# A planned order of work with a cap on open load requests and with new costs for some steps

## The chip, the cores and the metric

The kernel runs on one core of one Trainium2 chip. A core has five engines that this text names: TensorE (PE in the profile; PEld is its weight load), VectorE (DVE), ScalarE (ACT), GpSimd (POOL) and SyncE (SP), which issues DMAs. Each engine runs its own list of instructions in order, and waits for other engines through semaphores. The metric is the time of one execution on the device in microseconds (us). Before the change the median of three runs is 549.18 us (548.54 to 549.64).

## The reference

Cosine attention over 8 batches, 12 heads, 448 tokens and a head width of 64, followed by a mixer with a low-rank step over the tokens and an MLP over 768 channels:

```
q_n = q / (norm(q) + 1e-6);  k_n = k / (norm(k) + 1e-6)
attn = softmax(q_n @ k_n.T / tau);  x = attn @ v          # per head, then heads side by side: [8, 448, 768]
u = x + (x.T @ U @ V).T                                   # U [448, 32], V [32, 448]
out = u + relu(u @ w_ch1) @ w_ch2                         # 768 -> 3072 -> 768
```

Inputs and output are float32.

## The kernel before, in words

**Attention.** The batches are done one after another, in thirds of four heads and in pairs of heads. For a third, GpSimd issues one load of q and one of k (`load_qk`, line 588) into a ring of three, later two, buffers. `squares` (line 629) squares two heads at a time, on ScalarE (line 636), VectorE (line 640) or, for one third of batch 0, GpSimd (line 638), and VectorE sums each row of 64 (line 644). ScalarE and VectorE make the inverse norms (lines 658 to 666), VectorE multiplies q and k by them (line 712), and from batch 2 on a DMA transpose issued by SyncE (line 728) turns them. TensorE makes scores in bursts of three (line 776), ScalarE takes the exponentials (line 794), TensorE multiplies with v (line 821), and VectorE divides by the row sums (lines 852 and 853). v is loaded by GpSimd into two buffers, one for the even and one for the odd batches; from batch 1 on that takes six loads of line 611 and four of line 616, queued behind the six q and k loads of the same batch. A load of v waits for the values products of the batch that used the buffer before.

**Mixer and MLP.** TensorE projects (line 936) and expands (line 989), VectorE adds (line 998), and the tiles u of 128 tokens go to device memory and come back transposed through SyncE's queue. The MLP takes the first four tiles plainly (lines 1377 and 1419) and the other 24 in pairs with a scheme of seven block products in place of eight. For the first six pairs the first layer is plain (line 1265) and the second layer has seven products (line 1294); for the last six pairs both have (lines 1158 and 1294). The sums of blocks that the scheme needs are made by VectorE: of the second weights (`minus`), of the first weights (`rows_`, lines 1117 to 1120), of u (`cols_`), of the hidden layer (`sums_of`, `last_sums`), and of the products that lie in PSUM banks (line 1312). In each pair GpSimd adds u to a copy of one product for three blocks (line 1319), after ScalarE has made the copy (line 1317), and VectorE adds banks to these.

**What sets the order.** The order of the instructions on every engine is worked out while the kernel is built, by `Plan.run`. Each step is an `Op` with an engine (or a choice such as `"ACT/DVE"`), a cost in us, steps that it depends on, buffers that it takes (`acq`) and gives back (`rel`), and a priority. TensorE and GpSimd have several streams; a stream keeps its own order, and at each moment the first stream in a fixed ranking whose next step is ready is served. GpSimd's ranking is `pool_y` (the adds of line 1319), `pool_x`, `pool_q` (all loads), `pool_s`. TensorE ranks attention above the MLP. VectorE, ScalarE and SyncE take the ready step of lowest priority number; ScalarE leaves a `fast` step with a choice alone while VectorE is free:

```
if e == "ACT" and o.fast and "/" in o.eng and free["DVE"] <= t + 1e-9:
    continue
```

A load costs 0.71 us of GpSimd and ends later: the planner has one queue for loads, adds the load's `busy` time to it, and then its `late` time (`LATE` is 6.0 us; 11.0 for q and k from batch 3 on):

```
dma[q] = max(dma[q], o.end) + work
o.end = dma[q] + fixed
```

Buffers come from a `Ring`; one is free when the step that gave it back last has ended in the plan. When the planner is done, the instructions are written out in its order. The planner's times themselves are not in the program, and the waits between engines come from the data in the tiles. In batch 0, idle time that the plan shows for TensorE is filled with products that nobody reads (line 698).

Of the kernel before, what the change touches and what calls it, by code (L numbers as in the profile page):

```python
# [126 lines left out]

class Slot:
    def __init__(self, ring, uses):
        self.ring, self.uses, self.left, self.i, self.tile, self.last = ring, uses, uses, None, None, 0.0  # L130


class Op:
# [8 lines left out]
class Plan:  # L142
# [53 lines left out]
    def run(self):  # L196
# [26 lines left out]
        while left:  # L223
# [6 lines left out]
            while progress:  # L230
                progress = False
                for e in ("PE", "ACT", "POOL", "DVE", "SP"):
# [65 lines left out]
                                s.group = s.ring.take(s.i, t)  # L298
                    for s in o.rel:
                        s.left -= 1  # L300
                        s.last = max(s.last, o.end)
                        if s.left == 0:
                            s.ring.freed[s.i] = s.last
                    for c in kids.pop(o.seq, ()):
# [13 lines left out]
def kernel(  # L318
# [12 lines left out]
    nc = tc.nc  # L331
# [193 lines left out]
    def any_t(n, fast=1, fixed=0.065):  # L525
        return {"ACT": act_t(n), "DVE": dve_t(n, fast, fixed)}

    def load(fn, busy, deps=(), acq=(), rel=(), late=2.0):
        return plan.add(Op("POOL", 0.71, fn, deps=deps, acq=acq, rel=rel,
                           lat=("in", busy, late)), pool_q)  # L530

    def fill(fn, n=256, prio=8, acq=(), deps=()):
# [52 lines left out]
    def load_qk(b, h0, h1, ld=None, lo=0, uses=None):  # L585

        ld = ld or Slot(r_ld, 4 if uses is None else uses)
        ops = [load(lambda i=i, src=src: nc.gpsimd.dma_start(  # L588
            out=ld.tile[:, i, lo:lo + h1 - h0, :],
            in_=src[b, h0:h1].rearrange("h (s c) d -> s h (c d)", c=SC)),  # L590
            (h1 - h0) * (0.31 if b else 0.35) + (FIRST.get((h0, i), 0.0) if b == 0 else 0.0), acq=[ld], late=2.5 if b == 0 else LATE if b < 3 else 11.0) for i, src in enumerate((q, k))]
        return ld, ops, lo

    def key_rows(n0, n1):
# [8 lines left out]
    def load_v(b):  # L603

        old = [last_av.get((b - 2, p)) for p in range(NPAIR)] + (v_set[b] if WIDE <= b < WIDE + 2 else [])
        src = v[b].rearrange("h (s c) d -> c s h d", c=SC)
        if b < WIDE:
            ops = [load(lambda c=c: nc.gpsimd.dma_start(out=v_t[b % 2][0:SCH, :, c, 0:D], in_=src[c]),
                        SCH * H * 0.001, deps=old, late=LATE if b else VLATE) for c in range(SC)]
        else:  # L610
            ops = [load(lambda j=j, r0=r0, c=c, s0=s0, s1=s1: nc.gpsimd.dma_start(  # L611
                out=v_t[b % 2][r0:r0 + s1 - s0, :, j, 0:D], in_=src[c, s0:s1]),
                (s1 - s0) * H * 0.001, deps=old, late=LATE) for j, r0, c, s0, s1 in key_rows(0, 384)]
            (_, _, c, s0, s1), = key_rows(384, S)
            for e, hh in ((0, 0), (0, 1), (1, 0), (1, 1)):
                ops.append(load(lambda e=e, hh=hh, c=c, s0=s0, s1=s1: nc.gpsimd.dma_start(
                    out=v_t[b % 2][64 * e:64 * e + 64, 2 * e + hh::4, SC - 1, 0:D],
                    in_=src[c, s0:s1, 2 * e + hh::4]),
                    (s1 - s0) * H * 0.00025, deps=old, late=LATE))
        for h in range(H):  # L620
            got[b, h, "v"] = ops

    def squares(b, g, ld, ops, lo, ii, ss, pr, on, hold, then):

        red = []
        for i in ii:
            for a0 in range(0, g, G // 2):
                a1 = min(g, a0 + G // 2)
                sq = Slot(r_sq, 1)
                o = Op(on, 1.02 if on == "POOL" else 0.48 if on == "ACT" else 0.44, None,  # L630
                       deps=[ops[i], *hold], acq=[sq], prio=pr + 0.2, fast=True, port=True)
# [17 lines left out]
        return red  # L649
# [108 lines left out]
    def scores(b, slots, then=()):  # L758
# [26 lines left out]
        for (p, c), sc, (attn, exps) in zip(slots, scs, into):  # L785
            _, _, (inv, a, scaled) = sets[p]
            if (b, p) in RAW_KEYS:
# [12 lines left out]
    def values(b, p, X):  # L800
# [39 lines left out]
        for hh in range(2):  # L840
# [259 lines left out]
    def seven_rows(after, free):  # L1100
# [26 lines left out]
    def up_seven(tiles, relu, tops, ready, left, made_by, qk_free, s_free, z_free):  # L1127
# [8 lines left out]
            return qk_t[:, 384 * n:384 * (n + 1)].rearrange("p (i t) -> p i t", i=3)  # L1136

        def cols_(f, deps):
            return plan.add(Op("DVE", 0.15 + 384 * 0.00053, f, deps=deps, acq=[uT.slot], prio=-0.6, port=True))
# [49 lines left out]
        for k in (1, 6, 2, 7, 5, 3, 4):  # L1189
            for g in range(len(gs)):  # L1190
# [20 lines left out]
                elif k == 3:  # L1211
                    o = product(3, g, C_, False, [x["q22"]])
                    x["q12"] = op("DVE", PS, sum_op(blocks(g, 1), wide(z12[g]), C_, True), [o, x["z12"]], [relu], [z12[g], C_])
                    x["r12"] = op("DVE", 0.28, lambda g=g: nc.vector.tensor_relu(out=blocks(g, 1)(), in_=blocks(g, 1)()),
                                  [x["q12"]], prio=-0.4)
                else:
                    o = product(4, g, B_, False, [x["z22"]])
# [12 lines left out]
    def sums_of(js, relu, ready, r11, r12, r21, r22):  # L1230
# [2 lines left out]
        x = slice(js[0], js[-1] + 1)  # L1233

        def sums(f, deps, prio=0.1):
            return plan.add(Op("DVE", 0.15 + len(js) * 128 * 0.00053, f, deps=deps, acq=[relu], prio=prio, port=True))
# [6 lines left out]
    def last_sums(ready, *done):  # L1243

        Q, (S1, S2) = relu_views()
        for j0, o in zip((0, HF // 2), done):
            x = slice(j0, j0 + 6)
            d = plan.add(Op("DVE", 0.15 + 6 * 128 * 0.00053, lambda x=x: nc.vector.tensor_sub(
                S1[:, x], Q[:, x, 2], S2[:, x]), deps=[o, *(ready[j][6] for j in range(j0, j0 + 6))], prio=-0.55, port=True))
            for j in range(j0, j0 + 6):  # L1250
                ready[j][3] = d
# [1 line left out]
    def mlp_seven(tiles, right, made_by, up=None, after=()):  # L1253
# [52 lines left out]
        u1, u2 = us  # L1306

        def dve(f, deps, acq=(), rel=()):
            return plan.add(Op("DVE", 0.5, f, deps=deps, acq=acq, rel=rel, prio=-0.7))

        def bank(out, x, mm):
            return lambda: nc.vector.tensor_add(out=out(), in0=mm.tile[:, 0:CH], in1=x())
# [343 lines left out]
```

## Time and profile before

| | us |
|---|---|
| median of the runs | 549.18 (548.54 to 549.64) |
| the profiled execution, its own time | 548.87 |
| its span, first to last instruction | 547.1 |
| busy: TensorE, VectorE, ScalarE, GpSimd | 537.1, 448.3, 286.5, 141.3 |

The granted clock of TensorE is 1.000 over the span. One line of a group of instructions names the source line, the engine, the operation, what it writes and reads, the shapes, the count, then busy time and the mean of one in ns, then the engine's idle time just before them and what ended it. A line of the timeline gives the start, the duration, the engine, the line and the operation, with the number of instructions merged into it, and in brackets the engine's idle time before and its releaser. In the part on DMA issues the last number is the median time from issue to landing. The time of an instruction includes its latency, and the next one on the same engine can start before it has ended; the busy time of TensorE is modelled. A step of the program that begins at 100 us is at 100 us from the first instruction.

### The profile page before, as it was taken

How to read it: one execution, taken by the hardware profiler on the slowest of the kernel's cores; microseconds unless marked ns; L12 is line 12 of the kernel's file. 1: busy time of each engine (PE TensorE's matmuls, PEld its weight loads, DVE VectorE, ACT ScalarE, POOL GpSimd, SP SyncE). 2: the span in 40 equal slices, each digit the busy share in tenths (PEclk: the TensorE clock that was granted, in tenths of full speed). 3: DMA queues.
4: the chain of work that ended last, by engine and by line, in shares of the span. 5: the costliest groups of instructions: out<-in, count | busy, mean ns of one | idle time of the engine just before them, and what ended most of it. 6: DMA issues, size and time to landing. Idle time of an engine off the chain costs nothing.

```text
span 547.1 us, 15168 instructions
## 1 busy us (share of the span) xinstructions
PE 537.1 (98%) x6275; PEld 389.2 (71%) x6275; DVE 448.3 (82%) x1022; ACT 286.5 (52%) x470; POOL 141.3 (26%) x180
## 2 busy tenths in 40 slices
PE   7899999999999999999999999999999999999996
PEld 6565565677858757757757757868778787878783
DVE  8979959999897779979979987778968585858583
ACT  7976746566557765765765765542323131314140
POOL 8636233104220620621531430010202021111111
PEclk9999999999999999999999999999999999999999
DMA  9999999987947995986996593132041212122201
GB/s 154 201 206 137 204 204 185 157 119 106 127 119 118 109 162 105 165 140 111 125 179 128 94 153 85 44 80 57 19 139 30 87 32 88 30 87 32 81 8 59
DMA packets 142326, 61.11 MB, mean 112 GB/s; under 512 B 101009, under 2 KB 142257, under 8 KB 142257
## 3 DMA queue, kind: packets, MB, share of 16 engines
q0 software_dynamic: 72352, 25.73, 43.5%
q1 hardware_dynamic: 69904, 34.41, 28.7%
q8 instruction: 49, 0.80, 0.6%
q14 instruction: 21, 0.16, 0.1%
HBM read 56.93 MB, written 15.93 MB: 133 GB/s over the span
## 4 chain that ended last, share of the span: by engine, by line
PE 92%; DVE 5%; ACT 1%; POOL 1%; DMA 1%; issue 0%; DVEq 0%; POOLq 0%
PE bank L1294 29%; PE bank L1265 18%; PE bank L1158 15%; PE bank L821 8%; PE bank L776 6%; PE bank L1377 6%; PE bank L1419 6%; PE bank L989 2%; DVE qk_all L712 2%; DVE ss L644 1%; PE bank L936 1%; POOL sqk L638 1%; DMA relu<-in_q_dram 1%; PE bank L566 1%; DVE X_sb L859 0%
## 5 line engine op out<-in xcount | busy, mean ns | idle before, releaser
L794 ACT ACTIVATE attn<-bank 128x896 bf16<-128x896 f32 (+1 forms) x163 | 140.3, 916 | 40.6 <-PE bank L776 39.7
L1294 PEld LDWEIGHTS <-relu 128*128 128x128 bf16 x1008 | 95.9, 98 | 68.4 <-issue 8.8
L1265 PE MATMUL bank<-uT,w_sb 128*128 128x256 bf16 x864 | 103.4, 273 | 0.0
L1294 PE MATMUL bank<-w_sb,relu 128*128 128x384 bf16 x576 | 102.9, 326 | 0.0
L1265 PEld LDWEIGHTS <-w_sb 128*128 128x128 bf16 x864 | 81.9, 98 | 18.1 <-issue 7.6
L644 DVE TENSOR_REDUCE ss<-sqk 112x8 f32<-112x512 bf16 x96 | 62.3, 674 | 1.1 <-ACT sqk L636 0.7
L712 DVE TENSOR_TENSOR qk_all<-qk_all,inv 112x512 bf16<-112x512 bf16 x93 | 62.5, 707 | 0.2
L821 PEld LDWEIGHTS <-attn 128*128 128x128 bf16 (+1 forms) x1536 | 54.1, 97 | 6.7 <-issue 3.7
L588 POOL DMA_DIRECT2D qk_all<-in_q_dram x24 | 17.5, 728 | 158.8 <-ACT attn L794 79.2
L821 PE MATMUL bank<-v_nat,attn 128*128 128x65 bf16 (+1 forms) x1536 | 57.3, 193 | 0.9 <-DVE X_sb L859 0.7
L1158 PEld LDWEIGHTS <-w_sb 128*128 128x128 bf16 x864 | 49.3, 98 | 0.8
L1275 ACT ACTIVATE relu<-bank 128x512 bf16<-128x512 f32 x46 | 27.5, 597 | 41.1 <-PE bank L1265 39.2
L776 PE MATMUL bank<-sqk 64*64 64x448 bf16 (+1 forms) x460 | 46.9, 356 | 0.9 <-ACT sqk L1441 0.5
L1195 ACT COPY attn<-bank 128x512 f32<-128x512 f32 x18 | 10.5, 585 | 71.0 <-PE bank L1158 69.9
L1158 PE MATMUL bank<-uT,w_sb 128*128 128x128 bf16 x648 | 38.1, 219 | 0.0
L1186 ACT ACTIVATE relu<-relu 128x512 bf16<-128x512 bf16 x36 | 22.7, 630 | 29.5 <-DVE relu L1180 28.6
L636 ACT ACTIVATE sqk<-qk_all 112x512 bf16<-112x512 bf16 x55 | 33.6, 631 | 7.5 <-DVE ss L644 7.4
L611 POOL DMA_DIRECT2D v_nat<-in_v_dram x42 | 31.1, 750 | 17.8 <-DMA w_sb<-in_moe_w_ch_dram 12.9
L1377 PE MATMUL bank<-uT,w_sb 128*128 128x384 bf16 (+1 forms) x288 | 35.4, 273 | 0.0
L1419 PE MATMUL bank<-w_sb,relu 128*128 128x384 bf16 x192 | 35.0, 326 | 0.0
L853 DVE TENSOR_TENSOR X_sb<-bank,rd 128x256 bf16<-128x256 f32 x72 | 30.6, 425 | 2.5
L998 DVE TENSOR_TENSOR X_sb<-bank,X_sb 128x384 bf16<-128x384 f32 (+3 forms) x57 | 29.2, 543 | 0.9 <-PE bank L989 0.5
(132 smaller groups left out, 794.6 us busy)
## 6 DMA issues: line engine op xcount, KB each, us to landing
qk_all<-in_q_dram POOLq DMA_DIRECT2D x23, 224.0 KB, 5.7
qk_all<-in_k_dram POOLq DMA_DIRECT2D x23, 224.0 KB, 6.7
u_nat<-u SPq DMA_DIRECT2D x25, 192.0 KB, 3.0
w_sb<-in_moe_w_ch_dram POOLq DMA_DIRECT2D x4, 1152.0 KB, 18.4
w_sb<-in_moe_w_ch_dram POOLq DMA_DIRECT2D x8, 576.0 KB, 15.9
u<-X_sb SPq DMA_DIRECT2D x22, 192.0 KB, 1.9
v_nat<-in_v_dram POOLq DMA_DIRECT2D x11, 168.0 KB, 8.4
out_dram<-O_sb SPq DMA_DIRECT2D x11, 168.0 KB, 2.5
```

The source lines that it names most:

```text
L611: ops = [load(lambda j=j, r0=r0, c=c, s0=s0, s1=s1: nc.gpsimd.dma_start(out=v_t[b % 2][r0:r0 + s1 - s0, :, j, 0:D], in_=src[c, s0:s1]), (s ...
L636: nc.scalar.activation(out=y, in_=x, func=AF.Square)
L644: lambda i=i, a0=a0, a1=a1, sq=sq: nc.vector.reduce_sum(ss.tile[:, i, a0:a1, :].rearrange("p h c -> p (h c)"), sq.tile[:, 0:a1 - a0, :].re ...
L712: (nc.gpsimd if pool_ else nc.vector).tensor_mul(dst, src, sc)
L776: nc.tensor.matmul(out=out, lhsT=qkT.tile.rearrange("p b s -> p (b s)")[r, n0:n0 + w], rhs=qkT.tile[r, SC:2 * SC, :].rearrange("p c s -> p ...
L794: exps.append(plan.add(Op("ACT", act_t(2 * S, 0.08), lambda sc=sc, c=c, attn=attn: nc.scalar.activation(out=attn.tile[:, :, off:off + S] i ...
L821: nc.tensor.matmul(out=av.tile[:, t, 0:D + 1], lhsT=tail.tile[:, hh, 128 * t:128 * (t + 1)] if tail and j == SC - 1 else (attn if j < SC - ...
L1158: o = plan.add(Op("PE", pe_t(128), lambda i=i, j=j, jj=jj: nc.tensor.matmul(out=mm.tile[:, 128 * jj:128 * jj + 128], lhsT=left[k](i, j), r ...
L1265: o = plan.add(Op("PE", pe_t(256), lambda j=j, e=e, cc=cc, mm=mm: nc.tensor.matmul(out=mm.tile[:, 256 * e:256 * e + 256], lhsT=w1_sb[:, cc ...
L1294: o = plan.add(Op("PE", pe_t(CH), lambda j=j: nc.tensor.matmul(out=mm.tile[:, 0:CH], lhsT=left[k](j), rhs=right[k](j), start=(first and j ...
L1377: o = plan.add(Op("PE", pe_t(n), lambda cc=cc: nc.tensor.matmul(out=mm.tile[:, m:m + n], lhsT=w1_sb[:, cc, f * 128:(f + 1) * 128], rhs=uT. ...
L1419: nc.tensor.matmul(out=mm.tile[:, 0:c1 - c0], lhsT=relu.tile[:, f, i * 128:(i + 1) * 128], rhs=w2_t[:, f, c0:c1], start=(f == 0), stop=(f ...
```

## The change

It touches the planner's inputs. From batch 3 on, each load of q, k and v also takes one of eight slots of a new ring, `r_turn`, and gives it back when it ends. The slots have no tile. For q and k loads the slot counts as given back 5.0 us (`late - LATE`) before the load's own end, through the new field `soon`; for v loads the two ends are the same. Then the costs of some steps are other numbers: a square 0.52 us on ScalarE (0.48 before) and 0.34 on VectorE (0.44); an exponential has a fixed part of 0.058 (0.08); dividing by the row sums 0.55 (0.6); and the block sums of the seven-product scheme are all shorter.

```
 class Slot:
     def __init__(self, ring, uses):
-        self.ring, self.uses, self.left, self.i, self.tile, self.last = ring, uses, uses, None, None, 0.0
+        self.ring, self.uses, self.left, self.i, self.tile, self.last, self.soon = ring, uses, uses, None, None, 0.0, 0.0
...
-                        s.last = max(s.last, o.end)
+                        s.last = max(s.last, o.end - s.soon)
...
-    def load(fn, busy, deps=(), acq=(), rel=(), late=2.0):
-        return plan.add(Op("POOL", 0.71, fn, deps=deps, acq=acq, rel=rel,
+    r_turn = Ring(8, None)
+
+    def load(fn, busy, deps=(), acq=(), rel=(), late=2.0, b=0):
+        turn = [Slot(r_turn, 1)] if b >= 3 else []
+        for s in turn:
+            s.own, s.soon = True, max(0.0, late - LATE)
+        return plan.add(Op("POOL", 0.71, fn, deps=deps, acq=[*acq, *turn], rel=[*rel, *turn],
                            lat=("in", busy, late)), pool_q)
...
-                o = Op(on, 1.02 if on == "POOL" else 0.48 if on == "ACT" else 0.44, None,
+                o = Op(on, 1.02 if on == "POOL" else {"ACT": 0.52, "DVE": 0.34} if "/" in on else 0.52 if on == "ACT" else 0.34, None,
...
-            exps.append(plan.add(Op("ACT", act_t(2 * S, 0.08), lambda sc=sc, c=c, attn=attn: nc.scalar.activation(
+            exps.append(plan.add(Op("ACT", act_t(2 * S, 0.058), lambda sc=sc, c=c, attn=attn: nc.scalar.activation(
...
-                muls.append(plan.add(Op("DVE", 0.6, scale, deps=[o], acq=[rd, X], rel=[av, rd], prio=1)))
+                muls.append(plan.add(Op("DVE", 0.55, scale, deps=[o], acq=[rd, X], rel=[av, rd], prio=1)))
...
-            return plan.add(Op(eng, N * 0.00203 if eng == "POOL" else 0.15 + N * 0.00053, lambda: f(e), deps=deps, prio=prio,
+            return plan.add(Op(eng, N * 0.00203 if eng == "POOL" else 0.055 + N * 0.00053, lambda: f(e), deps=deps, prio=prio,
```

The three calls in `load_qk` and `load_v` (batches from 1 on) pass `b=b`. The remaining edits are of the kind of the last two: the fixed part of `cols_` 0.15 to 0.07, of `sums_of` 0.15 to 0.09, of `last_sums` 0.15 to 0.07, a relu on VectorE 0.28 to 0.21, and the additions of banks (`dve`) 0.5 to 0.48.

More of the change, by code (lines that the diff above doesn't have):

```diff
@@ L590, in load_qk @@
             in_=src[b, h0:h1].rearrange("h (s c) d -> s h (c d)", c=SC)),
-            (h1 - h0) * (0.31 if b else 0.35) + (FIRST.get((h0, i), 0.0) if b == 0 else 0.0), acq=[ld], late=2.5 if b == 0 else LATE if b < 3 else 11.0) for i, src in enumerate((q, k))]
+            (h1 - h0) * (0.31 if b else 0.35) + (FIRST.get((h0, i), 0.0) if b == 0 else 0.0), acq=[ld], late=2.5 if b == 0 else LATE if b < 3 else 11.0, b=b) for i, src in enumerate((q, k))]
         return ld, ops, lo
@@ L612, in load_v @@
                 out=v_t[b % 2][r0:r0 + s1 - s0, :, j, 0:D], in_=src[c, s0:s1]),
-                (s1 - s0) * H * 0.001, deps=old, late=LATE) for j, r0, c, s0, s1 in key_rows(0, 384)]
+                (s1 - s0) * H * 0.001, deps=old, late=LATE, b=b) for j, r0, c, s0, s1 in key_rows(0, 384)]
             (_, _, c, s0, s1), = key_rows(384, S)
@@ L618, in load_v @@
                     in_=src[c, s0:s1, 2 * e + hh::4]),
-                    (s1 - s0) * H * 0.00025, deps=old, late=LATE))
+                    (s1 - s0) * H * 0.00025, deps=old, late=LATE, b=b))
         for h in range(H):
@@ L1138, in cols_ @@
         def cols_(f, deps):
-            return plan.add(Op("DVE", 0.15 + 384 * 0.00053, f, deps=deps, acq=[uT.slot], prio=-0.6, port=True))
+            return plan.add(Op("DVE", 0.07 + 384 * 0.00053, f, deps=deps, acq=[uT.slot], prio=-0.6, port=True))
         a = cols_(lambda: nc.vector.tensor_sub(T(0), U()[:, :, 0, 1], U()[:, :, 0, 0]), ut + qk_free)
@@ L1213, in up_seven @@
                     x["q12"] = op("DVE", PS, sum_op(blocks(g, 1), wide(z12[g]), C_, True), [o, x["z12"]], [relu], [z12[g], C_])
-                    x["r12"] = op("DVE", 0.28, lambda g=g: nc.vector.tensor_relu(out=blocks(g, 1)(), in_=blocks(g, 1)()),
+                    x["r12"] = op("DVE", 0.21, lambda g=g: nc.vector.tensor_relu(out=blocks(g, 1)(), in_=blocks(g, 1)()),
                                   [x["q12"]], prio=-0.4)
@@ L1235, in sums @@
         def sums(f, deps, prio=0.1):
-            return plan.add(Op("DVE", 0.15 + len(js) * 128 * 0.00053, f, deps=deps, acq=[relu], prio=prio, port=True))
+            return plan.add(Op("DVE", 0.09 + len(js) * 128 * 0.00053, f, deps=deps, acq=[relu], prio=prio, port=True))
         a = sums(lambda: nc.vector.tensor_add(S1[:, x], Q[:, x, 1], Q[:, x, 3]), [*r12, *r22])
@@ L1247, in last_sums @@
             x = slice(j0, j0 + 6)
-            d = plan.add(Op("DVE", 0.15 + 6 * 128 * 0.00053, lambda x=x: nc.vector.tensor_sub(
+            d = plan.add(Op("DVE", 0.07 + 6 * 128 * 0.00053, lambda x=x: nc.vector.tensor_sub(
                 S1[:, x], Q[:, x, 2], S2[:, x]), deps=[o, *(ready[j][6] for j in range(j0, j0 + 6))], prio=-0.55, port=True))
@@ L1308, in dve @@
         def dve(f, deps, acq=(), rel=()):
-            return plan.add(Op("DVE", 0.5, f, deps=deps, acq=acq, rel=rel, prio=-0.7))
+            return plan.add(Op("DVE", 0.48, f, deps=deps, acq=acq, rel=rel, prio=-0.7))
         def bank(out, x, mm):
```

## The prediction

> **What bounds the kernel now.** I read the busy times and the chain first: if one engine is full, a new order can only win back its gaps.
>
> ```profile
> PE 537.1 (98%) x6275; PEld 389.2 (71%) x6275; DVE 448.3 (82%) x1022; ACT 286.5 (52%) x470; POOL 141.3 (26%) x180
> ...
> PE 92%; DVE 5%; ACT 1%; POOL 1%; DMA 1%; issue 0%; DVEq 0%; POOLq 0%
> ```
>
> TensorE is busy for 537.1 of 547.1 us and carries 92% of the chain. So I asked for the busy times by stage, to find where the other 10 us lie.
>
> ```profile
> 0.00:40.00 40.00, 34.95 (x487) 24.35 (x488) 33.77 (x101) 33.18 (x61) 23.54 (x35) 1.00 1.32 186
> 40.00:100.00 60.00, 59.93 (x584) 35.88 (x582) 52.10 (x123) 36.03 (x66) 22.42 (x32) 1.00 1.29 181
> 100.00:340.00 240.00, 239.41 (x2766) 169.55 (x2765) 210.51 (x486) 156.12 (x245) 67.62 (x93) 1.00 0.93 129
> 340.00:374.60 34.60, 34.60 (x416) 24.96 (x414) 27.75 (x67) 14.10 (x19) 2.65 (x3) 1.00 0.21 58
> ```
>
> The columns are the stretch, then the busy time of PE, PEld, DVE, ACT and POOL, then clock and DMA. The first 40 us lose 5.05 us of TensorE and hold besides the 147 filler products of line 698 (56 ns apart, 8.2 us). From 40 to 374.6 us TensorE is idle for 0.07 + 0.59 + 0.00 = 0.66 us in all. Nearly all of that, 13.00 - 12.42 = 0.58 us, lies between 318 and 331 us, and the timeline says why:
>
> ```profile
> 317.96 1.25 POOL L616 DMA_DIRECT2D v_nat<-in_v_dram  x2 [1.21 <-DMA v_nat<-in_v_dram]
> ...
> 319.23 0.92 POOL L1319 TENSOR_TENSOR relu<-relu,u_nat 128x384 f32<-128x384 f32 x1
> ...
> 320.18 0.56 DVE L1312 TENSOR_TENSOR relu<-bank,relu 128x384 f32<-128x384 f32 x1 [1.49 <-PE bank L776]
> ...
> 320.66 2.39 DVE L712 TENSOR_TENSOR qk_all<-qk_all,inv 112x512 bf16<-112x512 bf16 x2
> ...
> 322.97 0.54 DVE L1312 TENSOR_TENSOR O_sb<-bank,u_nat 128x384 f32<-128x384 f32 x1
> ...
> 323.57 0.97 PE L1294 MATMUL bank<-u_nat,relu 128*128 128x384 bf16 x5 [0.35 <-DVE O_sb L1312]
> ```
>
> GpSimd's add (L1319) stands behind the last two loads of v, and these stand in line for a landing. ScalarE's copy that the add needs ended at 316.18. The add ends at 320.15; only then can VectorE go on (it sat 1.49 us), everything behind it on VectorE is late, and TensorE waits 0.35 us for a bank at 323.57. Behind the start, a GpSimd load reaches TensorE here alone.
>
> **The change part by part.** No instruction is added or removed. The new slots of `r_turn` have no tile, so they make no wait on the chip; they hold a load back in the planner alone. All terms are therefore effects of another order.
>
> *The cap of eight.* From the issues and landings in the trace, the chip itself never has more than eight GpSimd loads open: in batches 3 to 7 the ninth and later ones stand waiting for a DMA.
>
> ```profile
> L616 POOL DMA_DIRECT2D v_nat<-in_v_dram x28 | 17.5, 629 | 19.1 <-DMA v_nat<-in_v_dram 6.7 <-DMA qk_all<-in_k_dram 5.1 <-DMA w_sb<-in_moe_w_ch_dram 4.8
> ...
> qk_all<-in_q_dram POOLq DMA_DIRECT2D x23, 224.0 KB, 5.7
> qk_all<-in_k_dram POOLq DMA_DIRECT2D x23, 224.0 KB, 6.7
> ```
>
> The question is whether the cap binds in the planner too. Twelve loads in a row (q, k, ten of v) cost it 12 x 0.71 = 8.5 us of GpSimd. With the cap the ninth waits for q's slot, which comes free at 0.71 + 4 x 0.31 + 6.0 = 7.95 us in place of 8 x 0.71 = 5.7 (the 11.0 us lateness counts as 6.0 for the slot); so it goes out 2.3 us later, and the next batch's q, by the same sum over the planner's DMA queue, about 12 us after the first q in place of 8.5. The trace has that distance at 11.3, 10.4, 13.3 and 15.9 us (130.46 to 141.80, 180.26 to 190.61, 219.32 to 232.62, 264.48 to 280.38). A rule speaks against any effect: the Trainium skill, "DMA: Bandwidth & Descriptors", section "Anatomy of one DMA", gives a GpSimd DMA 2.0 us plus its bytes at 436 GB/s; 224 KB would land in 2.5 us, at 0.71 us an issue only four would ever be open, no load would have to queue, and this term would be 0. The rows show 5.7 and 6.7 us for these loads and waits at the ninth, so I go by the rows: the cap binds.
>
> What it moves at 318 us: the add was ready at 316.18, which is 7.4 us after q's issue at 308.80. Under the cap the planner has GpSimd free between its eighth load (ends at 5.7) and its ninth (7.95), and again before each later one, so the adds (first stream of GpSimd, taken before loads) go ahead of the last two loads at least. Then the first add starts 1.25 us earlier, the VectorE add at 320.18 ends near 319.5 in place of 320.74, the two products of line 712 and the add of 322.97 move up by as much, and the bank is free near 322.3, before TensorE's 323.21. **Worth -0.35 us**, and -0.58 if all gaps of that stretch go; I take -0.4. Nothing else behind 40 us can be won: three other waits of VectorE for this add (2.62 us at 193.18, 0.44 at 234.34, 1.94 at 277.16) lie under TensorE's other products and cost it 0.
>
> A second rule speaks against the moved adds. The first of the three took 0.92 us at 319.23, but one at 392.50 took 1.79 us, and from 420 us on some take up to 2.57. The Trainium skill, "SBUF — State Buffer", section "Who interferes with whom", says that a VectorE instruction with two inputs in SBUF and a GpSimd one that reads SBUF exclude each other for a whole instruction. Squares and the products of line 712 are such. By the rule the moved add may take 0.87 us more; of the 1.25 us won 0.38 stay, the bank is free at 322.97 + 0.54 - 0.38 = 323.13, still before 323.21, and the term stays -0.35 with nothing to spare. By the rows all 18 adds before 374 us took 0.90 to 0.93, so I charge nothing.
>
> What is queued behind the held loads: on GpSimd the other loads, in the same order. With three adds of 0.91 us in front, the last two loads of v go out up to 2.7 us later and land near 327.5 in place of 324.8. The planner puts that batch's values products behind the later landing, and other products cover them: 0, and up to +2.7 once if that cover fails.
>
> *The next batch's first third of q and k.* Its loads are now laid some 3.6 us later, and everything made from them moves back in the lists: per third four squares and four sums, two small ScalarE and two small VectorE steps, four products of line 712, two DMA transposes on SP, whose queue holds also the stores and reloads of u; VectorE's share is 4 x 0.674 + 0.22 + 0.35 + 4 x 0.707 = 6.1 us. The cover is the slack that the list already gives it: the q issued at 190.61 landed at 196.94, and ScalarE squares come only at 204.76, so 7.8 us lay between. If nothing passes through, 0. If all of it passes in four batches, attention ends 4 x 3.6 = 14.4 us later. What that would cost is read at its end:
>
> ```profile
> 367.97 1.14 PE L821 MATMUL bank<-v_nat,attn 128*128 128x65 bf16 x32
> ...
> 371.75 0.95 DVE L1118 TENSOR_TENSOR qk_all<-X_sb,w_sb 128x1536 bf16<-128x1536 bf16 x1
> ...
> 374.47 2.17 PE L1158 MATMUL bank<-uT,w_sb 128*128 128x128 bf16 x36
> ```
>
> The last values products end at 369.11, TensorE has 5.4 us of other products before line 1158 begins, and the VectorE step that line 1158's second product needs (ends 372.70, used at 376.48) has 3.8 us to spare. So the first 3.8 us of lateness are free, and the rest up to 10.6 us is lost. By what it is nearest to, the row with 7.8 us of slack, I take 0.
>
> *The squares.* ScalarE has 55 in this form, VectorE 35. On the chip two on VectorE stand (1.09 - 0.417) / 2 = 0.34 us apart (three at 9.54 us), which is the new cost; the new 0.52 for ScalarE is near the 0.50 of the pair at 7.70 us. A cheaper VectorE is free earlier in the planner, and ScalarE takes a square only when VectorE is not free, so some of the 43 that ScalarE does between 100 and 340 us move. Ten of them would add 10 x 0.34 = 3.4 us to VectorE, which idles 29.5 us there, and take 5.2 us from ScalarE, which idles 84. TensorE: 0. If VectorE's idle time were in the wrong places, attention is late by at most those 3.4 us, inside the 3.8.
>
> *The other costs* (exponentials 0.824 to 0.802, row sums of 1536 elements 0.964 to 0.869, scaling 0.60 to 0.55 and so on) change no duration. Three exponentials in 2.54 us stand 0.81 us apart, and the 1536-element ones take 1.82 us for two, 0.87 apart: again the new numbers are the chip's. What they move cannot be read from the trace of before. A VectorE step one place too late costs at most the 0.71 us of the longest, of which the planner's margin of 0.5 us for TensorE covers all but 0.2: 0 to +2 for ten such places. I take 0.
>
> *The start.* Only squares and exponentials of batch 0 are touched here, but nothing covers it: TensorE waits for VectorE's products of line 712 (1.2 us in three waits) and its copies (0.8). One step of 0.6 to 0.7 us put before or behind another moves the start by that much; two such swaps give -1.4 to +1.4. I take 0.
>
> Sum: -0.4 + 0 + 0 + 0 + 0 = -0.4. The profiled execution took 548.87 us (span 547.1 and 1.8 around it), so 548.5 on its scale; it lies 0.3 below the median of 549.18, so 548.8 on the median's. I predict **548.7 us**. A measurement of this kernel tells about 0.2% (1.1 us; its runs lie within 548.54 to 549.64) from no change.
>
> **The rivals.** *Start laid better.* Two swaps win 1.4 us and the adds 0.6: 547.2 us. For it: 13 us of idle or filler there. Against it: the chain there is nearly all VectorE, which is busy 33.8 of 40 us. *Small waits.* The order of before leaves 0.66 us of waits in 335 us; one laid anew with shorter costs has less slack in each, and ten places of 0.2 us make 551.2 us with no gain. For it: TensorE has no other reserve. Against it: the new costs are those of the trace. *Attention late.* This is the mechanism of the first thirds; it decides when more than 3.8 us have added up by 369 us, and at 2.5 us in each of four batches costs 10 - 3.8 = 6.2 us: 555 us. For it: the lateness of 11 us stays in the loads while the held issue is now counted besides, so the same delay is laid twice. Against it: the 7.8 us of slack. *The cap doesn't bind where it should*, the adds stay behind the loads: 549.2 us, no change.
>
> **How the numbers follow.** The adds move and little else, or the cap does nothing: 0.30 (of it 0.04 faster, 0.24 within 0.2%, 0.02 slower; own range 547.9 to 549.9). Start better 0.26 (0.24 faster, 0.02 same). Small waits 0.28 (0.25 slower, 0.03 same). Attention late 0.16 (slower). Together faster 0.28, same 0.29, slower 0.43: the single likeliest time lies at no change, yet there is more room above it than below, since TensorE is full. Range 546.5 to 553.5: below it lies a start better still, above it most of the late attention, some 0.2 in all.
>
> **What would show it.** Right: in the changed profile the adds of line 1319 (their line moves by a few) come before the last two v loads near 318 us, TensorE's wait for VectorE there is gone, line 698 still has about 147 fillers, the first hidden-layer products start near 37.5 us, and line 1158's first product near 374 us. Start better or worse: that 37.5 moves by more than 0.5. Attention late: TensorE idles between the last values products and line 1158's. Small waits: TensorE's waits after 40 us add up to more than 1.5 us over several places. More squares on VectorE with no new wait of TensorE confirm their zero. What would make me wrong is a longer start, which no view of before can tell.

## The result and the profile after

The changed kernel takes **548.40 us** in the median of 20 runs (547.58 to 549.29), and the kernel before 549.11 us in 20 runs beside it (548.39 to 549.64). The ratio is **0.9987, 95% interval 0.9981 to 0.9993**: 0.7 us faster. That is inside the 0.2% that the prediction called no change, and yet clear of the noise, since the interval lies below 1. The forecast of 548.7 us was 0.3 us high. The profiled execution of the changed kernel took 547.75 us (span 546.0), 0.65 us below its own median.

In the changed kernel the lines from 530 on have moved down by five: the first-layer products of the last six pairs are L1163 (L1158 before), the adds of GpSimd L1324 (L1319), the additions of banks L1317 (L1312), the products with the inverse norms L717 (L712), the mixer's expansions L994 (L989), the row sums of the weights L1122 and L1123 (L1117 and L1118).

The busy times of the changed kernel and its chain by engine, from the page:

```profile
PE 537.7 (98%) x6276; PEld 390.2 (71%) x6276; DVE 448.7 (82%) x1033; ACT 280.7 (51%) x459; POOL 141.8 (26%) x180
...
PE 94%; DVE 3%; ACT 1%; POOL 1%; DMA 1%; issue 0%; DVEq 0%; POOLq 0%
```

Eleven instructions have gone from ScalarE (470 before, 459 now) to VectorE (1022, 1033). Eight of them are squares (55 on ScalarE and 35 on VectorE before, 47 and 43 now); the others are two relus of the hidden layer and a copy. TensorE's share of the chain is two points higher. The same stretches as before the change, in the same columns (PE, PEld, DVE, ACT, POOL, clock, DMA share, GB/s):

```profile
0.00:40.00 40.00, 35.99 (x489) 25.56 (x490) 33.81 (x101) 33.25 (x61) 24.08 (x35) 1.00 1.32 188
40.00:100.00 60.00, 60.00 (x580) 35.62 (x579) 50.89 (x122) 35.17 (x62) 22.80 (x34) 1.00 1.31 175
100.00:340.00 240.00, 240.00 (x2800) 170.49 (x2798) 215.66 (x506) 151.19 (x238) 67.14 (x92) 1.00 0.95 130
340.00:374.60 34.60, 34.60 (x405) 25.23 (x403) 25.93 (x60) 14.50 (x21) 2.66 (x3) 1.00 0.22 61
```

From 40 us on TensorE has no idle time left; before, it had 0.66 us. Where the 1.1 us between the two spans lie follows from the starts of three groups of products:

| stretch, us | before | after |
|---|---|---|
| start to the first hidden-layer product (L1377, L1382) | 37.49 | 37.35 |
| from there to the first product of L1158 (L1163) | 336.98 | 336.01 |
| from its first to its last product | 154.46 | 154.47 |
| from there to the end | 18.14 | 18.15 |

So 0.97 us come from the middle stretch, and 0.14 from the start. That start tells nothing: executions of kernels whose lists are the same up to there differ by 0.8 us in it (37.49 us in the kernel before, 38.32 in the kernel below with the sixth product later). At the place of the old stall, GpSimd and then VectorE of the changed kernel:

```profile
301.79 0.70 POOL L593 DMA_DIRECT2D qk_all<-in_q_dram  x1 [12.71 <-ACT attn L799]
...
310.96 1.34 POOL L621 DMA_DIRECT2D v_nat<-in_v_dram  x2 [2.08 <-DMA v_nat<-in_v_dram]
317.97 0.91 POOL L1324 TENSOR_TENSOR relu<-relu,u_nat 128x384 f32<-128x384 f32 x1 [5.66 <-ACT relu L1322]
```

```profile
319.36 0.56 DVE L1317 TENSOR_TENSOR relu<-bank,relu 128x384 f32<-128x384 f32 x1 [0.71 <-POOL relu L1324]
...
322.05 0.56 DVE L1317 TENSOR_TENSOR O_sb<-bank,u_nat 128x384 f32<-128x384 f32 x1 [0.71 <-PE bank L1299]
```

The adds did not go ahead of the last loads of v. The last q load of the last batch goes out at 301.79 us in place of 308.80, and the loads behind it were over 5.66 us before the adds came. VectorE now waits for TensorE at 322.05, no longer the other way round. The last values products of the attention start at 363.74 us in place of 368.92.

### The profile page after: what moved, and what is told of

Same layout as the page of the kernel before. It is cut to its first block, busy times and chain, and to the rows that moved or that the text cites. A ratio compares the mean times of both kernels' runs of the same rounds, so it can differ in the third digit from the quotient of the medians.

```text
span 546.0 us, 15182 instructions
## 1 busy us (share of the span) xinstructions
PE 537.7 (98%) x6276; PEld 390.2 (71%) x6276; DVE 448.7 (82%) x1033; ACT 280.7 (51%) x459; POOL 141.8 (26%) x180
## 4 chain that ended last, share of the span: by engine, by line
PE 94%; DVE 3%; ACT 1%; POOL 1%; DMA 1%; issue 0%; DVEq 0%; POOLq 0%
PE bank L1299 30%; PE bank L1270 18%; PE bank L1163 15%; PE bank L826 8%; PE bank L781 7%; PE bank L1382 6%; PE bank L1424 6%; PE bank L994 2%; DVE qk_all L717 1%; PE bank L941 1%; DVE ss L649 1%; POOL sqk L643 1%; DMA relu<-in_q_dram 1%; PE bank L571 1%; DVE X_sb L864 0%; ACT attn L794 0%
## 5 line engine op out<-in xcount | busy, mean ns | idle before, releaser
L717 DVE TENSOR_TENSOR qk_all<-qk_all,inv 112x512 bf16<-112x512 bf16 x93 | 60.7, 682 | 0.8 <-DMA sqk<-qk_all 0.5
L1163 PEld LDWEIGHTS <-w_sb 128*128 128x128 bf16 x864 | 49.3, 98 | 0.8
L1163 PE MATMUL bank<-uT,w_sb 128*128 128x128 bf16 x648 | 38.1, 219 | 0.0
L1382 PE MATMUL bank<-uT,w_sb 128*128 128x384 bf16 (+1 forms) x288 | 35.9, 273 | 0.0
L641 ACT ACTIVATE sqk<-qk_all 112x512 bf16<-112x512 bf16 x47 | 28.7, 631 | 9.8 <-DVE ss L649 9.7
```

Source lines behind the costliest of these rows:

```text
L717: (nc.gpsimd if pool_ else nc.vector).tensor_mul(dst, src, sc)
L1163: o = plan.add(Op("PE", pe_t(128), lambda i=i, j=j, jj=jj: nc.tensor.matmul(out=mm.tile[:, 128 * jj:128 * jj + 128], lhsT=left[k](i, j), r ...
L1382: o = plan.add(Op("PE", pe_t(n), lambda cc=cc: nc.tensor.matmul(out=mm.tile[:, m:m + n], lhsT=w1_sb[:, cc, f * 128:(f + 1) * 128], rhs=uT. ...
```

## The experiments

Every time below is a median, and each ratio is against runs of the kernel before on the same chip. The cap and the new costs can be taken apart, since both only steer the order.

**Is the stall at 323 us what was won?** Two kernels remove it in two ways that have nothing else in common. The first keeps the old costs and caps the loads of batch 7 alone:

```
-        turn = [Slot(r_turn, 1)] if b >= 3 else []
+        turn = [Slot(r_turn, 1)] if b >= 7 else []      # all costs as before the change
```

> Costs as before; the cap of eight only for batch 7's loads, so the order is that of before up to batch 7, and in GpSimd's list the three adds of that pair stand ahead of the last three loads of v. Theory A (the recorded prediction: adds stuck behind loads make TensorE's gap near 323 us): the first add starts near 316.5 to 318, TensorE's idle time between 318 and 331 us falls from 0.58 to under 0.1 us, time -0.4 to -0.6 us, ratio 0.9990. Theory B (the gain of the changed kernel comes from cheaper costs that bring attention forward, and the adds were not what TensorE's gap hung on): the gap stays at 0.35 to 0.58 us, ratio 1.0000, attention ends near 369 us. Theory C (each new order has small gaps of its own, and no part has a gain): TensorE's idle time behind 40 us is somewhere from 0 to 2 us, at other places than 323.

Measured: 547.92 us (547.75 to 548.87), ratio 0.9982 [0.9974, 0.9991]. GpSimd of this kernel:

```profile
314.58 0.63 POOL L621 DMA_DIRECT2D v_nat<-in_v_dram  x1
316.24 1.47 POOL L1324 TENSOR_TENSOR relu<-relu,u_nat 128x384 f32<-128x384 f32 x1 [1.03 <-ACT relu L1322]
317.67 1.78 POOL L1324 TENSOR_TENSOR O_sb<-relu,u_nat 128x384 f32<-128x384 f32 x2
319.39 1.89 POOL L621 DMA_DIRECT2D v_nat<-in_v_dram  x3
```

This is what the prediction described: the adds go ahead of the last three loads, and the stall is gone. One add took 1.47 us in place of 0.91, and that cost nothing. The second kernel leaves loads and costs as they were and puts that pair's three adds on VectorE:

```
-        y = [plan.add(Op("POOL", 1.0, ... nc.gpsimd.tensor_add(
+        y = [plan.add(Op("DVE" if ON_V else "POOL", 0.48 if ON_V else 1.0, ...
+            (nc.vector if ON_V else nc.gpsimd).tensor_add(          # ON_V: the pair whose adds ran at 319 us
```

> The kernel before (old costs, no cap), with the three adds of u of the fifth pair of tiles (those near 319 us, no others) done by VectorE in place of GpSimd, some 1.5 us more for VectorE; the order up to there is that of before. Theory A (the gap near 323 us comes from GpSimd's adds, late behind the loads and blocking VectorE): no product of line 717 over 1.3 us near 320, no gap of TensorE near 323, -0.4 to -0.6 us, ratio 0.9990. Theory B (TensorE's gap has another cause): 0.35 us or more idle near 323, ratio 1.000 or above. Theory C: another gap behind 320 us.

Measured: 548.18 us (547.67 to 548.55), 0.9985 [0.9976, 0.9993], no stall. In both kernels TensorE's products at 309 us stand within 0.03 us of where they stood in the kernel before, and all products from 374 us on stand 1.06 to 1.09 us earlier. So this one stall was worth 1.1 us in the profile, nearly twice the idle time that it shows there. TensorE of the kernel before:

```profile
321.75 1.46 PE L1294 MATMUL bank<-w_sb,relu 128*128 128x384 bf16 x8
323.57 0.97 PE L1294 MATMUL bank<-u_nat,relu 128*128 128x384 bf16 x5 [0.35 <-DVE O_sb L1312]
...
327.35 0.65 PE L821 MATMUL bank<-v_nat,attn 128*128 128x65 bf16 x16
328.16 0.65 PE L821 MATMUL bank<-v_nat,attn 128*128 128x65 bf16 x16 [0.16 <-ACT attn L794]
```

The last of the eight products of the first row starts at 322.89, and the next one 0.68 us later, where two such products otherwise start 0.16 us apart: 0.52 us lost, shown as 0.35. The first values products at 327.35 start 0.39 us after the product ahead of them (0.23 lost, shown as 0.07), and the second half 0.36 us after the last of the first, where 0.03 is usual (0.33 lost, shown as 0.16). Together that is 1.08 us, and the idle column has 0.58. The difference comes from how idle time is counted: it begins at the recorded end of the last product, which lasts 0.33 us in the record where the next one usually starts 0.16 us after it (0.19 and 0.03 for the values products). So each wait costs 0.16 to 0.17 us more than it shows.

**Which part of the change did it?** First the new costs without the cap (the slots are taken from batch 99 on, so never):

```
-        turn = [Slot(r_turn, 1)] if b >= 3 else []
+        turn = [Slot(r_turn, 1)] if b >= 99 else []     # all new costs stay
```

> The new costs without the cap. Theory A: the gain of the change is the cap's, so 549.1 us, ratio 1.0000, with the add behind the loads of v near 319 us and a gap of 0.35 us or more behind it. Theory B: last values products near 364 us in place of 369, batch 7's last q load near 302 us in place of 309, no gap of TensorE behind 40 us, -0.7 us, ratio 0.9987. Theory C: a gap somewhere, between -0.7 and +1.5 us.

Measured: 548.49 us (547.77 to 548.82), 0.9987 [0.9978, 0.9996], the ratio of the whole change; the middle stretch is 336.00 us (336.01 with the cap), and no gap is left (0.16 us at L994 that the view of waits still lists here is a product without a record: 59 products stand there beside 60 weight loads). Then the whole cap with the old costs:

```
         turn = [Slot(r_turn, 1)] if b >= 3 else []      # the cap as in the change
-                o = Op(on, ... {"ACT": 0.52, "DVE": 0.34} if "/" in on else 0.52 if on == "ACT" else 0.34, None,
+                o = Op(on, 1.02 if on == "POOL" else 0.48 if on == "ACT" else 0.44, None,   # and every other cost put back
```

> Costs as before, the whole cap (batches 3 to 7). Theory A: as e1, -0.4 to -0.6 us, ratio 0.9990, no gap near 323 us. Theory B: attention ends near 369 us as before, and the third loads of batch 7 go out near 308 us; ratio 1.0000. Theory C: gaps of 0 to 2 us elsewhere. The rival of the prediction (the first thirds pass their delay on): last values products at 372 to 380 us, and +0.5 to +6 us.

Measured: 551.52 us (550.54 to 552.25), **1.0045 [1.0033, 1.0057], slower**. The stall at 323 us is gone here too, but TensorE waits for row sums of the weights near 377 us:

```profile
PE bank L1163 <- DVE v_nat L1123: 1.2, 1, 1.2
PE bank L1163 <- DVE qk_all L1123: 0.6, 1, 0.6
```

So the costs carry the gain, and the cap alone loses 2.5 us in the medians. The trace shows less, 1.7 us (a span of 548.76 us against 547.07): the stretch of L1163 is 2.23 us longer, the middle stretch 1.20 shorter, and the start 0.63 longer. It is the trace of the fastest of five executions, at a granted clock of 0.998; the four others had 0.996 and took 1.3 us more in the median. What such an execution looks like is seen further down, in the kernel with the sixth product later. The costs were split next: the squares' two numbers alone, and all the others without them.

```
# e4: of the change, only this line
+                o = Op(on, ... {"ACT": 0.52, "DVE": 0.34} if "/" in on else 0.52 if on == "ACT" else 0.34, None,
# e7: every new cost but this line; no cap in either
```

> Only the costs of the squares are the new ones (0.52 and 0.34), no cap. Some 10 squares go from ScalarE to VectorE. Recorded zero for the squares: no gap of TensorE from VectorE's fuller list. In this order the adds of batch 7's pair stand ahead of three loads of v, so theory A says no gap near 323 us and -0.4 us. Theory B: attention ends 1 to 3 us earlier than 369, and the gain goes with it. Theory C: a gap somewhere, between -0.7 and +1.5 us.

> The new costs without those of the squares, no cap. If the earlier attention comes from the cheaper VectorE steps of the MLP and the shorter exponentials: last values products near 364 us and no gap behind 40 us, 548.5 us, ratio 0.9987, as with all costs. If it takes the squares too: values products end between 366 and 373, and a wait of line 1163 of up to 2 us where they end behind 371; ratio 1.000 to 1.006.

Measured: squares alone 552.31 us (550.97 to 554.24), **1.0059 [1.0043, 1.0075]**; the rest alone 547.50 us (547.09 to 548.69), 0.9975 [0.9964, 0.9986], 1 us under the 548.5 expected; its trace, of the slowest of seven executions (548.69), has two gaps of 0.2 us. Which of the other costs brings this was not tried. Only six squares move by the squares' costs alone, where some ten were expected. The squares' costs alone bring the same two waits as the cap alone, 1.25 and 0.64 us, and a new gap of 0.72 us at 279.46 us (and 0.16 us more just behind it):

```profile
275.90 2.71 DVE L669 TENSOR_SCALAR ln<-ln 112x32 f32<-112x32 f32 x1
275.90 0.92 POOL L1324 TENSOR_TENSOR relu<-relu,u_nat 128x384 f32<-128x384 f32 x1
...
276.78 1.78 POOL L1324 TENSOR_TENSOR O_sb<-relu,u_nat 128x384 f32<-128x384 f32 x2
...
278.91 0.49 DVE L1317 TENSOR_TENSOR relu<-bank,relu 128x384 f32<-128x384 f32 x1
...
279.46 1.78 PE L1299 MATMUL bank<-w_sb,relu 128*128 128x384 bf16 x10 [0.72 <-DVE relu L1317]
```

L669 is a small step that otherwise takes 0.17 us. Here it begins together with the first of three adds of GpSimd and ends at 278.61, 0.05 us after the last of them; the addition of a bank that stands behind it frees TensorE's bank too late.

**What makes the row sums late?** The prediction had put this at the end of the attention. The first trial took the products that need the row sums a little later in the pairs, on top of the whole cap with the old costs:

```
-        for k in (1, 6, 2, 7, 5, 3, 4):
+        for k in (1, 2, 6, 7, 5, 3, 4):
```

> As e2 (whole cap, old costs), and in the last six pairs the products of the first layer come as 1, 2, 6, 7, 5, 3, 4 in place of 1, 6, 2, 7, 5, 3, 4, so that the sixth product, for which TensorE stood 1.25 + 0.64 us in e2, is asked for 36 products (2.0 us) later. Theory D (late attention: the values products end too late for VectorE's sums of the first weights): both gaps near 377 us are gone, time 1.5 to 2.2 us under e2, so 549.3 to 550.0. Rival E (e2's loss lies in its other gaps or its start, and the wait only moves to the next product): a wait of 1 us or more on line 1163 remains and the time is within 0.5 us of e2's.

Measured: 551.73 us (551.10 to 553.32), 1.0057 [1.0045, 1.0069]. Nothing was won: the waits moved to the next block sum (L1124), 1.65 and 0.64 us near 386 us. The trace, of the slowest of its six executions (553.32 us, granted clock 0.997), shows besides what a lower mean clock stands for. First a row of the stretches, with the clock third from the end, then TensorE:

```profile
388.00:392.00 4.00, 4.00 (x47) 4.00 (x46) 2.21 (x4) 0.00 (x0) 0.00 (x0) 0.59 0.02 4
```

```profile
387.40 3.55 PE L1163 MATMUL bank<-uT,attn 128*128 128x128 bf16 x35 [0.64 <-DVE attn L1124]
```

Behind the two waits, 32 products start 0.107 us apart in place of 0.056, which costs 1.6 us more. In this kernel, the cap alone and the squares alone, 9 of 17 executions had a clock of 0.996 or 0.997, and they took 1.3 to 1.6 us longer in the median than the rest of the same kernel; in all other kernels, the one before included, 6 of 182 had less than 0.998. So waits of about 2 us in a row seem to be paid a second time in about half of the executions. That the waits bring the lower clock is read from this one trace and these counts, and was not tested. It is part of the medians of these three kernels.

The kernel with three adds on VectorE gave the hint on the row sums. Its last values products start as late as those of the cap alone, and it has no wait:

```profile
356.56 0.32 PE L994 MATMUL bank<-A_sb,V_sb 128*128 128x384 bf16 x1
...
370.97 1.14 PE L826 MATMUL bank<-v_nat,attn 128*128 128x65 bf16 x32
...
373.40 2.17 PE L1163 MATMUL bank<-uT,w_sb 128*128 128x128 bf16 x36
```

```profile
363.87 0.33 PE L994 MATMUL bank<-A_sb,V_sb 128*128 128x384 bf16 x1
...
369.52 0.33 PE L994 MATMUL bank<-A_sb,V_sb 128*128 128x384 bf16 x1
370.66 1.14 PE L826 MATMUL bank<-v_nat,attn 128*128 128x65 bf16 x32
...
377.33 0.23 PE L1163 MATMUL bank<-qk_all,v_nat 128*128 128x128 bf16 x1 [1.25 <-DVE v_nat L1123]
```

The first fence is the kernel with adds on VectorE, the second the cap alone, both TensorE. What differs is batch 6's mixer: its last expansions (L994) run at 356.56 in the one and at 363.87 and 369.52 in the other (354.97 in the kernel before, 356.06 after the change). The row sums are written over the mixer's tile X, so they must wait until X is stored. To test this, batch 6's expansions of the first column half were put into the higher TensorE stream, that of the values products, in the kernels with the squares' costs alone and with the cap alone:

```
-  ..., pe_a if c1 < C or jobs is wide else pe_av)
+  ..., pe_a if (c1 < C and b != 6) or jobs is wide else pe_av)
```

> The same ranking of batch 6's first L994 expansions on top of e4_squares (552.31 us: only the two squares costs changed, no cap). Theory F: the waits of the first L1158 product go, the L1158 stretch falls from 156.69 to 154.5, and about 0.9 us of loss stays, since the gap of 0.72 us near 279 behind a VectorE operation that took 2.7 us under GpSimd's adds has another cause: 550.0 to 550.6. Rival (the end of the attention is the gate): 552.3 within 0.4.

> The kernel before with the whole cap and the old costs (as in e2_cap, 551.52 us), and batch 6's mixer expansions of the first column half (L994) ranked with the values products instead of below them. Theory F (what is late in e2_cap, e4_squares and e5_cap_sixth_later is batch 6's mixer step: L994 at 363.9 and 369.5 us instead of 349 to 356, so that the last rows sums L1122 and L1123 come at 375 to 377): L994 goes back to before 360, the first L1158 product no longer waits for L1123, the L1158 stretch goes from 156.69 back to 154.5, and the time falls by 1.9 to 2.5 us against e2_cap, to 549.0 to 549.6. Rival (the end of the attention at 371.6 us is the gate itself): the waits of 1.25 and 0.64 us stay, and the time is 551.5 within 0.4.

Measured with the squares' costs: 549.28 us (548.96 to 549.62), 1.0004 [0.9996, 1.0013] in place of 1.0059. The waits for row sums are gone, although the attention ends later than in any kernel above (its last values product starts at 376.5 us; 371.6 in the cap alone, 372.7 in the squares alone):

```profile
348.15 0.49 PE L994 MATMUL bank<-A_sb,V_sb 128*128 128x384 bf16 x2
...
375.57 1.14 PE L826 MATMUL bank<-v_nat,attn 128*128 128x65 bf16 x32
```

So for this kernel theory F, the mixer, is shown, and the attention's end as the gate is refuted. The stall near 279 us stays, as expected (0.96 us, and 0.16 behind it). The stretch of L1163 is 156.41 us and not the 154.5 expected, since values products now lie inside it; the sum of the waits is the better measure. The time fell by 3.0 us in the medians where about 1.9 was expected. In the traces, from the first hidden-layer product to the end, it is 2.13 us (512.05 to 509.92), and 2.1 us against the three executions of the squares alone at a clock of 0.999 (median 551.42); the rest belongs to its three executions with a lower clock. With the whole cap: 549.88 us (549.57 to 550.41), 1.0017 [1.0009, 1.0026] in place of 1.0045, 0.3 us above the expected span. The waits for L1123 are gone, but one of 1.68 us for L1124 has come, so that from the first hidden-layer product to the end the traces differ by 0.33 us only (510.64 and 510.31); the rest of the 1.6 us between the medians lies in the start and in the four executions of the cap alone with a lower clock:

```profile
383.11 1.87 DVE L1185 TENSOR_TENSOR relu<-bank,v_nat 128x512 bf16<-128x512 f32 x3
384.90 0.94 DVE L1124 TENSOR_TENSOR attn<-w_sb,qk_all 128x1536 bf16<-128x1536 bf16 x1
```

The last block sum stands behind six additions of products on VectorE (L1185, from 381.31 us on, the last three in the fence); in the kernel with the squares' costs it runs ahead of these six, at 380.96. Here the theory holds for the row sums and not for the whole loss; that the order of VectorE's list alone makes this last wait is read from the trace and was not tried.

**Are the squares better left on ScalarE?** The changed kernel with the squares' two old costs was run twice, the second time beside the changed kernel itself on one chip:

```
-                o = Op(on, ... {"ACT": 0.52, "DVE": 0.34} if "/" in on else 0.52 if on == "ACT" else 0.34, None,
+                o = Op(on, 1.02 if on == "POOL" else 0.48 if on == "ACT" else 0.44, None,
```

> The changed kernel with the squares' costs as before (0.48 and 0.44). As e7: near 548.5 us with the values products ending near 364 us, if the other costs carry the gain; 549 to 552 us and values products ending from 369 on, if the squares do.

> The changed kernel once more, beside e12 on the same chip. All theories: 0.9987 of before within 0.0006, near 548.3 us, no idle of TensorE over 0.1 us between 40 and 370 us.

> The changed kernel with the squares' costs put back to 0.48 (VectorE) and 0.44 (ScalarE), once more. If leaving the squares on ScalarE is worth something on top of the rest of the change: 0.9975 of before within 0.0006, 0.6 to 0.8 us below e11_after_again. Rival (both have TensorE without a gap, so they are equal and e8_after_old_squares was a lucky set of executions): within 0.2 us of e11_after_again.

(The last expectation has the two engines exchanged: the old costs are 0.48 for ScalarE and 0.44 for VectorE, as in the edit.) Measured: 547.62 us (547.05 to 547.75), 0.9975 [0.9964, 0.9986]; on the shared chip 547.83 us (547.08 to 548.21), 0.9979 [0.9969, 0.9989], beside 548.22 us (547.77 to 548.69), 0.9987 [0.9978, 0.9995] for the change. The difference of 0.4 us lies between the two expectations and the intervals overlap. In the profiles it is hardly there: from the first hidden-layer product to the end this variant takes 508.03 and 508.07 us in place of 508.63 and 508.61, but that product comes 0.35 to 0.55 us later. It beats the kernel before; that it beats the changed kernel is not settled.

## Why the prediction was right, and where it was not

1. **The stall was the whole gain, as predicted; its size was too small.** The term was -0.35 us, -0.58 at most, read from the idle column. The two kernels that remove only this stall gain 1.06 to 1.09 us in the profile, and the loss counted from start to start is 1.08. By the ratios they gain 1.0 and 0.8 us (0.9982 and 0.9985, intervals from 0.4 to 1.4 us). The mis-sized term is this one.

2. **The stall was the right place, but in the changed kernel the cap did not remove it, and so the number was in part luck.** That the cap binds and puts the adds ahead of the last loads is shown by the kernel with the cap for batch 7. In the changed kernel the new costs had moved the whole attention of the last batches forward, and the adds met an idle GpSimd. The new costs without the cap give the same ratio and the same middle stretch: there the costs, priced at nothing, won what the cap was to win. The sign that the prediction named, adds ahead of the last two v loads, did not appear.

3. **"The next batch's first third: 0" failed for the cap by itself.** With the old costs the cap costs 2.5 us in the medians against the kernel before (1.7 in the trace): alone it would have been a clear loss. The gate of the prediction was right: the VectorE row sums for L1158's second block product, with 3.8 us to spare. In the kernel with the cap alone they start at 377.19 in place of 371.75, 5.4 us late, and TensorE waits 1.9 us, which lengthens the stretch by 2.23. What feeds the gate was wrong: not the end of the attention but batch 6's mixer step, which stands below the values products in TensorE's ranking. The changed kernel escaped: its expansions run until 356.4 us, as those of the kernel before do (355.3).

4. **"The squares: 0" and "the other costs: 0" failed in the same way.** About ten squares were expected to move; eight did in the changed kernel, six by their costs alone and five by the other costs alone. The squares' costs alone make the kernel 0.6% slower, and the other costs alone make it 0.25% faster. Zero was right for neither part, and that the sum of all terms came out near the measured time is luck. Each new set of numbers draws a new order, and whether it ends early or late is decided by single places that no duration in the trace of before tells.

5. **The lock between VectorE and GpSimd was charged on one side only.** I read GpSimd's adds, found all at 0.90 to 0.93 us, and took the price as nothing. VectorE was the one that waited. The products of line 712 between 100 and 340 us, with minimum, median and maximum in ns, before the change:

```profile
L712 DVE TENSOR_TENSOR qk_all<-qk_all,inv x68: 673/684/1784, 99.8 to 332.3; 112x512 bf16<-112x512 bf16 x68
```

   and after it:

```profile
L717 DVE TENSOR_TENSOR qk_all<-qk_all,inv x64: 677/684/692, 108.2 to 331.7; 112x512 bf16<-112x512 bf16 x64
```

   Before, the first of the two products at 320.66 took 1.78 us, and ended 0.56 us after GpSimd's run of adds did (322.44 and 321.88). So VectorE lost 1.1 us by this lock and 1.49 by the late add before the step at 322.97 that TensorE waited for; by arithmetic the absence of either would have closed the gap, and no run separates the two. The rule of the Trainium skill, "SBUF — State Buffer", section "Who interferes with whom", is that whichever issues first holds the ports for its whole instruction and the other blocks. That one blocks the other agrees with these rows, with VectorE as the loser in the costly cases. The order does not follow from it: the product of 320.66 waited for the rest of one add and also for the next, which began at 320.97.

6. **The start: 0** held: 37.35 against 37.49 us, 148 fillers against 147. A shift of 0.5 us, the sign named for it, would have proved nothing beside the 0.8 us by which executions with the same lists differ. **The rows against the DMA rule** held as well: loads of 224 KB take 5.5 and 6.3 us in the median, not the 2.5 worked out from the page.

7. **The rivals.** Small waits: refuted, no wait of TensorE above 0.1 us is left after 40 us. Start laid better: not seen. The cap does nothing: true of the cap inside the changed kernel, since without it the costs give the same time. Attention late: its loss is real in two half versions of the change, with another cause. Its price of 6.2 us was too high; the largest loss measured in a median was 3.3 us, with a stall of another kind and executions at a lower clock in it; the two waits themselves cost 2.23.

## What to carry to other kernels

When a change alters the numbers that a planner works with, cost its parts together and apart: here the cap and the squares' costs each lose half a per cent alone, and yet the whole change with both in it gains, so a zero for the sum says nothing of the parts. Count a stall from start to start of the products around it and not by the idle column, and follow the gate of a later stage back to the lowest-ranked step that feeds it. When two engines exclude each other, read the durations on both sides. When the medians of a kernel move more than its trace, look at the granted clock of each execution.

## What the hardware showed that was not expected

A VectorE step that meets a run of GpSimd adds can wait for the whole run and not for one instruction only: the 0.17 us step above took 2.71 us under three adds in a row (2.66 us together), at two places of that kernel, and the product of 0.68 us took 1.78 at two places of the kernel before, each time until 0.05 to 0.56 us after the last add. It is not always so: in the kernel with the cap alone a product that met the first add near 233 us took 1.43 us and got in ahead of the second add, which then took 1.36 us in place of 0.91. What decides between the two was not tested.

Second, after two waits of TensorE of 1.65 and 0.64 us close together, the trace of one kernel has its products at half their pace for 3.4 us (0.107 us apart in place of 0.056), at a granted clock of 0.59 over the stretch from 388 to 392 us.
